# Re-laying the first chunks of an mLSTM cell that feeds a squared-ReLU FFN

## The chip, the cores and the metric

The kernel runs on one core of a Trainium2 chip, as one program. The metric is the device time of one execution in microseconds (us). The engines that matter are TensorE (PE in the profile, with its weight loads as PEld), VectorE (DVE), ScalarE (ACT), GpSimd (POOL) and SyncE (SP), which issues nearly all DMA transfers. Each works through its own instructions strictly in the order in which the kernel lists them, and waits on the others by semaphores.

## The reference

Four sequences with eight heads of 40 elements run through an mLSTM cell over 768 steps. What comes out, 3072 tokens of 320 elements, goes through an FFN with 2048 hidden units.

```python
for t in range(768):                                   # q, k, v, o: (4, 8, 768, 40); gates: (4, 8, 768)
    m_new = max(f[t] + m, i[t])
    f_stab, i_stab, m = exp(f[t] + m - m_new), exp(i[t] - m_new), m_new
    C = f_stab * C + i_stab * outer(v[t], k[t])
    n = f_stab * n + i_stab * k[t]
    y[t] = sigmoid(o[t]) * (C @ q[t]) / max(abs(n @ q[t]), 1)
x = y.transpose(0, 2, 1, 3).reshape(3072, 320)
h = maximum(x @ w_in, 0)                               # w_in: (320, 2048), double precision words
out = (h * h) @ w_out                                  # w_out: (2048, 320)
```

## The kernel before

**Chunks.** The 768 steps of a sequence are cut into six chunks of 128, so there are 24 chunks s in all. Within a chunk the recurrence is a masked, weighted attention, and from chunk to chunk a state C is carried. For each chunk the kernel turns k and q with TensorE (`transposes`, L417, copied out of PSUM in L420), multiplies them (`scores`, L429), forms the weights W as the exponential of a decay row A plus a bias (`weigh`, L391), multiplies scores and weights (`weighted`, L444), and then, in `attend`, multiplies the old state with q (`hi`, L453), forms the new state's addition (`dC`, L460), and multiplies the weighted scores with v (`hp`, L467). `normalise` (L589 to L599) divides by the denominator and applies the output gate, and `turn_rows` (L629, L630) turns the result for the FFN.

**Gates.** A comes from the forget and input gates of all 32 rows (sequence, head) and 768 steps at once: `do_gates` (L252 to L261) runs two scans and six elementwise instructions on VectorE, and `turn_gates` brings the bias `b_T` and the factor `eA_T` into the other layout. A chunk needs A spread over all 128 partitions. For chunks 0 and 1 `spread_A` does that with TensorE: per half of the heads one 512 wide f32 matmul that writes the causal mask (L354) and four 128 wide matmuls that add the rows (L358). From chunk 2 on A goes to DRAM (`a_rows`, L916), comes back by a broadcasting DMA (`A_bc`, L342), and POOL applies the mask (`mask`, L367).

**Rounding of the weights.** w_in and w_out arrive as 64 bit words. Eighteen pieces are fetched through four buffers (`raw`, L193), each fetch being issued when the piece four before it has been joined. A piece takes two ScalarE instructions (`words`: L202, L204), three on VectorE (`join`: L213, L217, L218), and one 32 bit integer addition on POOL (L222). The first FFN group needs pieces 0 to 2, the second 3 and 4, the third 5 to 7, the fourth 8 and 9.

**FFN.** `ffn1_main` (L651) multiplies 256 tokens (two chunks) with 512 columns of w_in, and `ffn1_rest` (L662) adds the last 64 rows; four such groups make one 256 token block. `relu_half` (L675) and `square_half` (L681) follow on ScalarE. Later blocks use forms with fewer products (L742, L816, L848).

**Order.** The order on each engine is written out by hand: a list of calls for the front (L896 to L955), then a loop u = 0 to 7 that mixes chunks 2 to 5 with eight FFN groups, then a loop over all remaining parts. `idle(n)` (L883) issues n matmuls of zeros that nobody reads: twelve at the start, and 4, 3, 4 and 4 later.

```python
    do_gates()
    rounding.words()
    nc.scalar.dma_start(A_d[:, :], A_sb[:])
    spread_A(0)
    ...
    spread_A(1)
    scores(1, (True, True))
```

Of the kernel before, what the change touches and what calls it, by code (L numbers as in the profile page):

```python
# [17 lines left out]
P = 128  # L18
# [11 lines left out]
def kernel(  # L30
# [60 lines left out]
    conv = brought.enter_context(tc.tile_pool(name="conv", bufs=2, side="right"))  # L91

# [18 lines left out]
    later = gates.tile([P, P], F32)  # L111

# [4 lines left out]
    def make_consts():  # L117
        for t in kq_b:
            nc.vector.memset(t[:, :, :, D:], 0.0)
        for t in va_b:  # L120
            nc.vector.memset(t[:, :, D:], 1.0)
        for t in va_w:
            nc.gpsimd.memset(t[:, H * D1 :], 0.0)
        nc.vector.memset(keep[:], 1.0)
        nc.vector.memset(keep[:, :, 0:1], 0.0)
        make_identity(nc, ident[:])

        nc.gpsimd.memset(sel[:], 0.0)
        nc.gpsimd.affine_select(
            sel[:], sel[:], compare_op=ALU.not_equal, fill=1.0, base=0, pattern=[[-1, H], [0, P]], channel_multiplier=1,  # L130
        )

        nc.gpsimd.memset(later[:], 0.0)
        nc.gpsimd.affine_select(
            later[:], later[:], compare_op=ALU.is_ge, fill=-1e30, base=0, pattern=[[1, P]], channel_multiplier=-1,
        )

        nc.gpsimd.memset(bdm[:], 1.0)
        nc.gpsimd.memset(bdm[:DP, :, 1, :], 0.0)
        nc.gpsimd.memset(bdm[DP:, :, 0, :], 0.0)  # L140
# [29 lines left out]
    class Rounding:  # L170
# [36 lines left out]
        def join(self):  # L207
# [14 lines left out]
            nc.gpsimd.tensor_tensor(dst.bitcast(I32), bits, low.bitcast(I32), op=ALU.add)  # L222
# [24 lines left out]
    def load_gates():  # L247
        nc.sync.dma_start(f_sb[:], f_gate.rearrange("b h s -> (b h) s"))
        nc.scalar.dma_start(i_sb[:], i_gate.rearrange("b h s -> (b h) s"))

    def do_gates():
        nc.vector.tensor_tensor_scan(m_sb[:], f_sb[:], i_sb[:], -1e30, op0=ALU.add, op1=ALU.max)  # L252
        nc.vector.memset(f_sb[:, 0:1], 0.0)
        nc.vector.tensor_tensor(f_sb[:, 1:], f_sb[:, 1:], m_sb[:, : S - 1], op=ALU.add)
        nc.vector.tensor_tensor(f_sb[:, 1:], f_sb[:, 1:], m_sb[:, 1:], op=ALU.subtract)
        nc.vector.tensor_scalar_max(f_sb[:], f_sb[:], LOG_ZERO)
        nc.vector.tensor_tensor_scan(
            A_sb[:], keep[:].rearrange("p c t -> p (c t)"), f_sb[:], 0.0, op0=ALU.mult, op1=ALU.add,
        )
        nc.vector.tensor_tensor(i_sb[:], i_sb[:], m_sb[:], op=ALU.subtract)  # L260
        nc.vector.tensor_tensor(i_sb[:], i_sb[:], A_sb[:], op=ALU.subtract)  # L261

    def turn_gates():
        for src, dst in ((i_sb, b_T), (A_sb, eA_T)):
            tp = ps_o.tile([P, W], F32, name="tp", tag="o_ps")[:, : S // P * BH].rearrange("p (c r) -> p c r", r=BH)
            for c in range(NB):
                nc.tensor.transpose(tp[:, c, :], src[:, c * P : (c + 1) * P], ident[:BH, :BH])
            nc.scalar.activation(
                dst[:].rearrange("p b c h -> p c b h"), tp.rearrange("p c (b h) -> p c b h", b=B),
                AF.Copy if dst is b_T else AF.Exp,  # L270
            )
# [74 lines left out]
    def spread_A(s):  # L346

        b, c = divmod(s, NB)
        H2 = H // 2
        d = st.setdefault(s, {})  # L350
        d["A"] = []
        for i in range(2):
            A = ps_h.tile([P, H2, P], F32, name="A_ps", tag="h_ps")
            nc.tensor.matmul(  # L354
                A[:], lhsT=ident[:], rhs=later[:].unsqueeze(1).to_broadcast([P, H2, P]), start=True, stop=False,
            )
            for h in range(H2):
                nc.tensor.matmul(  # L358
                    A[:, h, :], lhsT=sel[:, i * H2 + h, :], rhs=A_sb[:, c * P : (c + 1) * P],
                    start=False, stop=(h == H2 - 1),  # L360
                )
            d["A"].append(A)
# [16 lines left out]
    def weigh(s, masked=False):  # L379
        b, c = divmod(s, NB)  # L380
        d = st[s]
        A, n = d["A"], H // len(d["A"])
        d["W"] = flat_c[:, H * P * (s % 2) : H * P * (s % 2 + 1)].rearrange("p (h t) -> p h t", t=P) if s < W_IN else A[0]
        if s < X_SQ:
            d["dec"] = prep.tile([P, H], F32, name="dec")
        if len(A) == 1 and not masked:
            mask(s)
        for i in range(len(A)):
            hh = slice(i * n, (i + 1) * n)
            for h in range(n):  # L390
                nc.scalar.activation(  # L391
                    d["W"][:, i * n + h, :], A[i][:, h, :], AF.Exp, bias=b_T[:, b, c, i * n + h : i * n + h + 1],
                )
            if s < X_SQ:
                nc.scalar.activation(d["dec"][:, hh], A[i][:, :, P - 1], AF.Exp)
        values(s)
# [14 lines left out]
    def transposes(s, o=(False, False)):  # L411
        d = st[s]
        kqT(s)
        for i, n in enumerate(("kT", "qT")):
# [5 lines left out]
            (nc.scalar.copy if i == 0 or s in (0, *range(2, 7)) else nc.vector.tensor_copy)(d[n], tp)  # L420
# [25 lines left out]
    def attend(s):  # L446
        b, c = divmod(s, NB)
        d = st[s]
        C = st.get("C")
        if c > 0:  # L450
            hi = ps_at.tile([P, H, D1], F32, name="hi", tag="at")
            for j in range(PR):
                nc.tensor.matmul(  # L453
                    hi[:, 2 * j : 2 * j + 2, :].rearrange("p h d -> p (h d)"), lhsT=d["qT"][:, j, :],
                    rhs=C[:, j].rearrange("p h d -> p (h d)"), start=True, stop=True,
                )
        if c + 1 < NB:
            dC = ps_at.tile([P, PR, 2, D1], F32, name="dC", tag="at")
# [6 lines left out]
        hp = d["hp"] = ps_at.tile([P, H, D1], F32, name="hp", tag="at")  # L465
        for h in range(H):
            nc.tensor.matmul(  # L467
                hp[:, h, :], lhsT=d["P"][h % 2][:, h // 2, :], rhs=d["va"][:, h, :], start=True, stop=True,
            )
        d["num"] = hp  # L470
        if c > 0:
            num = d["num"] = old.tile([P, H, D1], F32, name="num", bufs=1)
            nc.vector.tensor_tensor(
                num[:], hi[:], eA_T[:, b, c, :].unsqueeze(2).to_broadcast([P, H, D1]), op=ALU.mult,
            )
        if c + 1 < NB:
            Cn = old.tile([P, PR, 2, D1], F32, name="C_sb")
            nc.vector.tensor_tensor(Cn[:], dC[:], bdm[:], op=ALU.mult)
            if c > 0:
                Cd = old.tile([P, H, D1], F32, name="Cd", bufs=1)  # L480
                nc.gpsimd.tensor_tensor(
                    Cd[:], C[:].rearrange("p j i d -> p (j i) d"),
# [4 lines left out]
            st["C"] = Cn  # L487

# [96 lines left out]
    def normalise(s):  # L585
# [4 lines left out]
        dm = work.tile([P, H], F32, name="dm")  # L590
# [3 lines left out]

        x = d["x"] = work.tile([P, 3 * P], F32, name="x_sb")
        x3 = x[:, :DM].rearrange("p (h d) -> p h d", d=D)
        nc.vector.tensor_tensor(x3, num[:, :, :D], d["og"], op=ALU.mult)
        nc.vector.tensor_tensor(x3, x3, dm[:].unsqueeze(2).to_broadcast([P, H, D]), op=ALU.mult)
        nc.vector.tensor_copy(x[:, DM:], x[:, DM - KR : DM])  # L599

# [39 lines left out]
    def ffn1_main(g, pp):  # L640

        if pp == 0:
            new_g2(g)
        xT = st["xT", g]

        hs = [ps_h.tile([P, 2, WG], F32, name="h_ps") for _ in range(2)]
        for i in range(2):
            for n in range(2):
                fb = 4 * pp + 2 * n + i
                for a in range(2):  # L650
                    nc.tensor.matmul(  # L651
                        hs[i][:, n, :], lhsT=w_in[:, a, fb * P : (fb + 1) * P], rhs=xT[:, :, a, :],
                        start=(n == 0 and a == 0), stop=False,
# [225 lines left out]

    def idle(n):  # L880
        t = ps_h.tile([P, W], F32, name="idle", tag="h_ps")
# [14 lines left out]
    load_gates()  # L896
    load_part(0, 0)
    load_part(0, 1)
    fetch(2)
    make_consts()  # L900
    load_part(1, 0)
    load_part(1, 1)
    load_part(0, 2)
    fetch(1)
    load_o(0)
    load_o(1)
    load_part(1, 2)
# [3 lines left out]
    idle(4)  # L911
    scores(0)
    idle(3)
    do_gates()
    rounding.words()
    nc.scalar.dma_start(A_d[:, :], A_sb[:])  # L916
    spread_A(0)
    rounding.words()
    turn_gates()
    rounding.join()  # L920
    weigh(0)
    transposes(1, (False, True))
    spread_A(1)
    scores(1, (True, True))
    weigh(1)
    first.close()
    ffn = ctx.enter_context(tc.tile_pool(name="ffn", bufs=2))
    before = ExitStack()
    old = before.enter_context(tc.tile_pool(name="old", bufs=2))
    weighted(0)  # L930
    weighted(1)
    load(2)
# [5 lines left out]
    attend(0)  # L938
    rounding.step()
    normalise(0)  # L940
    mask(2)
    attend(1)
    normalise(1)
    load(3)
    load_A(3)
    rounding.step()
    turn_rows(0)
    idle(4)
    transposes(2)
    idle(4)  # L950
    sigmoid(2)
    sigmoid(3)
    turn_rows(1)
    weigh(2, masked=True)
    rounding.step()  # L955
# [3 lines left out]
    for u in range(8):  # L959
        s = 2 + u // 2  # L960
        relu_half()
        if u % 2 == 0:
            if u == 0:
                ffn1(0, 0)
                scores(s)
                rounding.step()
            else:
                turn_rows(s - 1)
                scores(s)
                ffn1(u // 4, u % 4)  # L970
            if u == 2:
                rounding.words()
# [7 lines left out]
            else:  # L980
                weigh(s + 1)
                square_half()
        else:
            load_A(s + 2)
            for r in {1: (4,), 3: (5, 6), 5: (7,), 7: ()}[u]:
                load(r)
# [4 lines left out]
            if u == 3:  # L991
                square_half()
# [12 lines left out]
            square_half()  # L1005
# [5 lines left out]
    square_half()  # L1011
# [134 lines left out]
```

## Time and profile before

| | |
|---|---|
| median of 12 runs | 514.0 us (512.96 to 515.07) |
| the profiled execution's own time | 515.07 us |
| its span, first to last instruction | 513.3 us |
| PE busy / PEld busy | 504.3 us / 462.4 us |
| DVE, ACT, POOL busy | 346.9, 248.4, 113.6 us |
| mean granted TensorE clock | 0.992 |

The profiled execution is the slowest of the twelve. Outside its span lie 515.07 - 513.3 = 1.77 us. A row of the timeline gives the start, the length, the engine, the line, what is written and read, the number of like instructions merged, and in brackets how long the engine had been idle and what ended that. In a table of stretches each row is a piece of the span with the busy time of each engine in it, the share of the TensorE clock that was granted (PEclk), and the use of the DMA engines. PE's busy time counts a matmul until its result is out, so a busy PE isn't PE at its peak. All times in the text are counted from the start of the span.

### The profile page before, as it was taken

To read this page: it belongs to the slowest core of one execution; us is meant where nothing else is said; L and a number is where in the kernel's file an instruction comes from. 1 tells how busy PE (TensorE), PEld (TensorE's weight loads), DVE (VectorE), ACT (ScalarE), POOL (GpSimd) and SP (SyncE) were. 2 spreads that over 40 slices of the span, in tenths; PEclk is the share of its full clock that TensorE was granted. 3 is DMA by queue.
4 is the path that set the end of the run, shared out by engine and by line. 5 is a ranking of instruction groups with operands and counts; after the bars stand their busy time and mean duration, and the time that the engine had idled before them with its cause. 6 is when DMAs were issued, how large, how long until landed. Compare 5 with 4: busy or idle time off the path is not lost.

```text
span 513.3 us, 11843 instructions
## 1 busy us (share of the span) xinstructions
PE 504.3 (98%) x4649; PEld 462.4 (90%) x4649; DVE 346.9 (68%) x630; ACT 248.4 (48%) x492; POOL 113.6 (22%) x138
## 2 busy tenths in 40 slices
PE   9989999999999999999999999999999999999997
PEld 4868878787798999999999999999999999999997
DVE  8589866663879776668668767667669667644341
ACT  3767888745440641680651780550771641432400
POOL 3345643232013122112112131112112112020000
PEclk9997999999999999999999999999999999999999
DMA  9999899845574785685675785785755353100000
GB/s 194 219 220 204 247 234 185 166 105 107 119 162 91 177 157 113 167 158 116 161 144 110 182 151 112 175 162 92 172 122 113 96 115 86 44 10 28 0 27 27
DMA packets 238231, 67.63 MB, mean 132 GB/s; under 512 B 185600, under 2 KB 232704, under 8 KB 238176
## 3 DMA queue, kind: packets, MB, share of 16 engines
q1 hardware_dynamic: 238080, 66.68, 62.0%
q8 instruction: 37, 0.61, 0.5%
q10 hardware_dynamic: 96, 0.20, 0.1%
q14 instruction: 18, 0.15, 0.1%
HBM read 54.56 MB, written 17.86 MB: 141 GB/s over the span
## 4 chain that ended last, share of the span: by engine, by line
PE 89%; DVE 4%; DMA 2%; issue 2%; ACT 1%; SPq 1%; DVEq 0%
PE h_ps L742 32%; PE h_ps L816 21%; PE h_ps L651 7%; PE h_ps L848 7%; PE tp L429 4%; PE h_ps L688 3%; PE numT L528 3%; PE h_ps L662 2%; PE hp L467 2%; PE numT L519 2%; DMA A_bc<-a_rows 1%; PE tp L417 1%; PE dC L460 1%; PE A_ps L358 1%; PE dC L538 1%
## 5 line engine op out<-in xcount | busy, mean ns | idle before, releaser
L367 POOL TENSOR_SCALAR_AFFINE_SELECT A_bc<-A_bc 128x1024 f32<-128x1024 f32 x22 | 27.7, 1258 | 212.2 <-ACT kq L377 136.2
L742 PE MATMUL h_ps<-T,S 128*128 128x160 f32 x352 | 51.4, 299 | 0.0
L391 ACT ACTIVATE A_bc<-A_bc,b_T 128x128 f32<-128x128 f32 x144 | 44.0, 388 | 10.8 <-POOL A_bc L367 10.4
L742 PE MATMUL h_ps<-w_out,g 128*128 128x160 f32 x336 | 49.2, 303 | 0.0
L742 PEld LDWEIGHTS h_ps<-T,S 128*128 128x128 f32 x352 | 49.0, 190 | 0.0
L377 ACT ACTIVATE kq<-A_bc 64x512 f32<-64x512 f32 x30 | 18.9, 629 | 61.7 <-DMA A_bc<-a_rows 61.5
L651 PE MATMUL h_ps<-xT,w_in 128*128 128x256 f32 x192 | 45.7, 394 | 1.6 <-ACT xT L630 1.6
L742 PEld LDWEIGHTS h_ps<-w_out,g 128*128 128x128 f32 x336 | 46.1, 190 | 1.1
L651 PEld LDWEIGHTS h_ps<-xT,w_in 128*128 128x128 f32 x192 | 36.9, 197 | 7.6 <-ACT xT L630 2.0
L816 PE MATMUL h_ps<-xT,w_in 128*128 128x128 f32 x288 | 40.7, 285 | 0.5 <-ACT r_sb L829 0.5
L829 ACT COPY r_sb<-h_ps 128x512 f32<-128x512 f32 x18 | 10.5, 584 | 61.3 <-PE h_ps L816 61.3
L758 DVE TENSOR_TENSOR y_sb<-y_sb,h_ps 128x160 f32<-128x160 f32 x44 | 14.0, 319 | 36.2 <-PE h_ps L742 36.2
L816 PE MATMUL h_ps<-xs,w_in 128*128 128x128 f32 x288 | 38.1, 275 | 0.0
L816 PEld LDWEIGHTS h_ps<-xT,w_in 128*128 128x128 f32 x288 | 34.9, 191 | 3.5 <-ACT r_sb L829 0.7
L848 PE MATMUL h_ps<-xT,w_in 64*128 64x128 f32 x432 | 36.9, 281 | 0.0
L848 PEld LDWEIGHTS h_ps<-xT,w_in 64*128 64x128 f32 x432 | 33.4, 188 | 2.2
L816 PE MATMUL h_ps<-xs,WS 128*128 128x128 f32 x288 | 35.1, 275 | 0.0
L816 PEld LDWEIGHTS h_ps<-xs,w_in 128*128 128x128 f32 x288 | 35.0, 192 | 0.0
L816 PEld LDWEIGHTS h_ps<-xs,WS 128*128 128x128 f32 x288 | 33.6, 192 | 0.0
L853 DVE TENSOR_TENSOR r_sb<-r_sb,h_ps 128x512 f32<-128x512 f32 x18 | 12.4, 687 | 26.7 <-PE h_ps L848 26.7
L545 DVE STREAM_TRANSPOSE tn<-numT 128x256 f32<-128x256 f32 x36 | 15.8, 449 | 21.1 <-PE numT L528 21.1
L444 DVE TENSOR_TENSOR A_bc<-tp,A_bc 128x512 f32<-128x512 f32 x36 | 23.1, 684 | 9.5 <-PE tp L429 9.5
(168 smaller groups left out, 1069.5 us busy)
## 6 DMA issues: line engine op xcount, KB each, us to landing
A_bc<-a_rows SPq DMA_DIRECT2D x22, 512.0 KB, 4.7
raw<-in_moe_w_out_dram SPq DMA_DIRECT2D x8, 640.0 KB, 4.4
num_rows<-tn SPq DMA_DIRECT2D x18, 256.0 KB, 3.5
kq<-num_rows SPq DMA_DIRECT2D x72, 64.0 KB, 2.5
kqT<-kq_rows SPq DMA_DIRECT2D x34, 128.0 KB, 3.2
raw<-in_moe_w_in_dram SPq DMA_DIRECT2D x8, 512.0 KB, 5.5
kq<-in_k_dram SPq DMA_DIRECT2D x24, 160.0 KB, 5.0
va<-in_v_dram SPq DMA_DIRECT2D x24, 160.0 KB, 5.1
```

The lines of the kernel that those rows point to most:

```text
L367: nc.gpsimd.affine_select(A[:], A[:], compare_op=ALU.is_ge, fill=-1e30, base=0, pattern=[[0, H], [1, P]], channel_multiplier=-1,)
L377: nc.scalar.activation(e[rows], st[s]["A"][0][rows, PR * i : PR * (i + 1), :], AF.Exp)
L391: nc.scalar.activation(d["W"][:, i * n + h, :], A[i][:, h, :], AF.Exp, bias=b_T[:, b, c, i * n + h : i * n + h + 1],)
L429: nc.tensor.matmul(sc[i][:, j, :], lhsT=d["kT"][rows, j, :], rhs=d["qT"][rows, j, :], start=True, stop=True,)
L444: nc.vector.tensor_tensor(t, d["sc"][i], d["W"][:, heads, :], op=ALU.mult)
L528: nc.tensor.matmul(numT[i][halves[g], e, :], lhsT=va_w[s % NKQ][:, h * D1 : h * D1 + DP], rhs=d["P"][h % 2][:, h // 2, :] if s < KQ_SQ els ...
L545: nc.vector.transpose(to[:, 2 * i : 2 * i + 2], numT[i][:, :2, :].rearrange("p c t -> p (c t)"))
L651: nc.tensor.matmul(hs[i][:, n, :], lhsT=w_in[:, a, fb * P : (fb + 1) * P], rhs=xT[:, :, a, :], start=(n == 0 and a == 0), stop=False,)
L688: nc.tensor.matmul(o_ps, lhsT=st["g2", g][:, fb, j * P : (j + 1) * P], rhs=w_out[:, fb, :], start=(fb == 0), stop=(fb == NF - 1),)
L742: nc.tensor.matmul(to, lhsT=lhsT[:, p], rhs=rhs[:, p, :], start=(start and p == 0), stop=(p == NPAIR - 1), skip_group_check=True,)
L816: nc.tensor.matmul(to[:, n, :], lhsT=lhsT[:, 4 * q + n, :], rhs=rhs, start=(start and n == 0), stop=True, skip_group_check=True,)
L848: nc.tensor.matmul(to[:, n, :], lhsT=w_in2[rows, 4 * q + n, :], rhs=rhs, start=False, stop=True, skip_group_check=True,)
```

## The change

The work per chunk and per weight piece stays the same; what changes is the order of the first four chunks and how some steps are done.

- The gates are computed and loaded in two parts (`SPANS`): first the 256 steps of chunks 0 and 1, then the other 512, with one elementwise instruction less. Each part is stored to `a_rows` by itself, now from SP's queue, not ACT's.
- Chunk 0's A is still spread by TensorE, but the mask matmul is in bf16. Chunk 1's A comes by `load_A(1)` and `mask(1)`, as for later chunks; its ten matmuls go. Both copies of `transposes` are always on ScalarE.
- `attend` and `normalise` are cut into pieces, which the front calls one by one; `weigh` can be done in two halves.
- The first FFN group is multiplied in two halves of 128 tokens, chunk 0's before chunk 1's.
- The fillers stand elsewhere: twelve at the start, then 3, 2, 1, 2, 2 and 2, all into one PSUM bank.
- The rounding's last step goes from POOL to VectorE. There it becomes one instruction over 16 bit halves: 128x1024 elements for a piece of 512 words, 128x1280 for one of 640.
- Weight pieces are fetched later in SP's queue (piece 0 behind the first store of A, piece 1 behind `load_A(1)`), and the loop begins at u = 2.

```diff
@@ constants
+    later_h = gates.tile([P, P], BF16)
+    ident_h = gates.tile([P, P], BF16)
+        nc.vector.tensor_copy(ident_h[:], ident[:])
+        nc.vector.tensor_copy(later_h[:], later[:])
@@ join
-            nc.gpsimd.tensor_tensor(dst.bitcast(I32), bits, low.bitcast(I32), op=ALU.add)
+            nc.vector.tensor_tensor(dst.bitcast(I32), bits, low.bitcast(I32), op=ALU.add)
@@ gates
+    FIRST = 2
+    SPANS = (slice(0, FIRST * P), slice(FIRST * P, S))
+    def load_gates(part):
+        cols = SPANS[part]
+        nc.sync.dma_start(f_sb[:, cols], f_gate.rearrange("b h s -> (b h) s")[:, cols])
+        nc.scalar.dma_start(i_sb[:, cols], i_gate.rearrange("b h s -> (b h) s")[:, cols])
+    def gates_floor(part):     # scan, subtract, add, clamp
...
+    def gates_sum(part):       # scan, one max-and-add
...
+    def turn_gates(part):
...
@@ spread
+    def spread_mask(s):
+        d = st.setdefault(s, {})
+        d["A"] = [ps_h.tile([P, PR, P], F32, name="A_ps", tag="h_ps") for _ in range(2)]
+        for A in d["A"]:
+            nc.tensor.matmul(
+                A[:], lhsT=ident_h[:], rhs=later_h[:].unsqueeze(1).to_broadcast([P, PR, P]), start=True, stop=False,
+            )
+    def spread_A(s, i):
...
@@ transposes
-            (nc.scalar.copy if i == 0 or s in (0, *range(2, 7)) else nc.vector.tensor_copy)(d[n], tp)
+            nc.scalar.copy(d[n], tp)
@@ attend
+    def attend(s):
+        from_C(s)
+        to_C(s)
+        from_chunk(s)
+        decayed(s)
+        next_C(s)
@@ normalise
+    def normalise(s):
+        denominators(s)
+        gated(s)
@@ ffn1_main
-    def ffn1_main(g, pp):
+    def ffn1_main(g, pp, half=None):
...
+                        hs[i][:, n, cols], lhsT=w_in[:, a, fb * P : (fb + 1) * P], rhs=xT[:, js, a, :],
...
@@ the front, whole up to chunk 2
+    load_gates(0); load_part(0, 0); load_part(0, 1); load_gates(1); make_consts()
+    gates_floor(0); gates_sum(0); load_part(0, 2); load_part(1, 0); load_part(1, 1)
+    store_A(0); fetch(1); load_o(0); load_A(1); load_part(1, 2); fetch(1); load_o(1); fetch(1)
+    idle(12); transposes(0); spread_mask(0); idle(3); spread_A(0, 0); turn_gates(0); idle(2)
+    spread_A(0, 1); idle(1); scores(0); weigh(0); gates_floor(1); mask(1); weighted(0); gates_sum(1)
+    load_part(2, 0); load_part(2, 1); store_A(1); fetch(1); transposes(1, (True, True))
+    rounding.words(); from_chunk(0); idle(2); to_C(0); turn_gates(1)
...
+    rounding.join(); denominators(0); next_C(0); idle(2); scores(1, (True, True))
+    rounding.words(); weigh(1, masked=True); rounding.join()
+    load_part(2, 2); load_A(2); load_o(2); load_o(3); sigmoid(0); sigmoid(1)
+    rounding.words(); weighted(1); to_C(1); from_C(1); from_chunk(1); idle(2)
+    gated(0); decayed(1); turn_rows(0); mask(2); transposes(2); normalise(1); next_C(1)
+    ffn1_main(0, 0, 0); rounding.words(); turn_rows(1)
...
+    scores(2); ffn1_main(0, 0, 1); ffn1_rest(0, 0, st["half"][0])
...
-    for u in range(8):
+    for u in range(2, 8):
```

(In the front above several calls share a line; in the file each has its own.)

## Prediction

> **What bounds the kernel now.** I first read the page's busy shares and its 40 slices, then a table of stretches, then the timeline of the first 70 us.
>
> ```profile
> PE 504.3 (98%) x4649; PEld 462.4 (90%) x4649; DVE 346.9 (68%) x630; ACT 248.4 (48%) x492; POOL 113.6 (22%) x138
> ```
>
> PE is busy nearly throughout. So the question is at which time PE gets into the dense part, and what it does before that. The stretches:
>
> ```profile
> 15.00:21.00 6.00, 6.00 (x44) 4.12 (x43) 2.49 (x4) 5.05 (x21) 1.19 (x2) 1.00 1.08 249
> 21.00:30.00 9.00, 8.74 (x71) 7.54 (x70) 8.32 (x20) 5.97 (x12) 4.25 (x5) 1.00 1.14 213
> 30.00:41.00 11.00, 8.82 (x65) 7.59 (x66) 8.98 (x15) 6.84 (x16) 5.72 (x5) 1.00 0.92 197
> 41.00:48.00 7.00, 7.00 (x28) 6.37 (x28) 6.25 (x12) 6.80 (x17) 4.12 (x5) 0.52 1.29 228
> 48.00:62.00 14.00, 14.00 (x102) 11.68 (x102) 12.21 (x19) 10.93 (x24) 8.52 (x8) 1.00 0.77 232
> ```
>
> The third number is PE, the fifth DVE, and the third from the end the granted clock. From 41 us on PE is always busy, with a few us idle in the remaining 450 (70 to 95 us: 25.00 of 25.00). From the third FFN group on both kernels issue the same matmuls, so what the front gains or loses by then is the change in the time. Second, from 21 us to 62 us DVE is the other full engine: 8.32 + 8.98 + 6.25 + 12.21 = 35.8 of 41 us. Third, between 41 and 48 us PE ran at half its clock. The timeline shows what went before that, and what DVE does there:
>
> ```profile
> 39.46 1.09 PE L460 MATMUL dC<-vw,kq 128*128 128x82 f32 x8 [1.07 <-DVE g_c L444]
> 40.39 2.76 PE L467 MATMUL hp<-va,g_c 128*128 128x41 f32 x16
> 42.95 1.95 PE L417 MATMUL tp<-ident,kq 128*128 128x128 f32 x8
> ...
> 49.48 1.32 POOL L222 TENSOR_TENSOR w_in<-mag,low 128x512 int32<-128x512 int32 x1 [1.72 <-ACT mag L202]
> 49.70 1.38 DVE L217 TENSOR_SCALAR mag<-mag 128x512 int32<-128x512 int32 x1
> ```
>
> PE stood idle for 1.07 us, with small matmuls on both sides, and about 2 us later L417 took 1.95 us where it took 1.09 us at 14.13. And L217, which takes 0.43 us alone (12.33), takes 1.38 us when it starts under a POOL addition. The forms of DVE's groups give the sum (the first 70 us):
>
> ```profile
> L217 DVE TENSOR_SCALAR mag<-mag 128x512 int32<-128x512 int32 x10 | 8.1, 808 | 0.3
> L218 DVE SCALAR_TENSOR_TENSOR mag<-raw,mag 128x512 int32<-128x512 int32 x10 | 6.9, 692 | 0.3
> ```
>
> Ten L217 cost 8.1 us where 10 x 0.43 = 4.3 would do, so POOL's additions cost DVE 3.8 us here, and 0.95 us more at L599 (46.65, 1.15 us against 0.20): 4.75 us.
>
> **The change, part by part.** *TensorE's share.* Chunk 1's spread goes (1.02 + 1.16 + 1.13 + 1.15 = 4.5 us), and chunk 0's two f32 mask matmuls (1.02 and 1.13) become two bf16 ones, at 0.22 each by the fillers of the same shape (four in 1.03 with the drain): 1.7 us less. The halves of the first FFN group cost nothing: 8 half-wide products take about 1.9 us (L816, 16 records in 1.95) against 3.72 for 8 full ones. Three fillers fewer: 0.7 us. About 6.9 us of PE work go, but I credit none of it in the main sum, since by my ledger DVE sets when PE may go on; if DVE didn't, it would count in full (first rival).
>
> *Chunk 1's weights.* This is a new path, and the longest. The gates' loads are there by about 3.9 us (L252 started at 4.06 with all columns; DVE is free at 3.5 and has two small copies more). Part 0 takes a third of 1.75 + 0.94 + 0.95 + 0.55 + 1.75 us, with some fixed time: 2.3 us; A is ready at 6.2. Then the store and the load, each from issue to landing; the first 30 us have rows for both:
>
> ```profile
> A_bc<-a_rows SPq DMA_DIRECT2D x2, 512.0 KB, 5.3
> a_rows<-A_sb ACTq DMA_DIRECT2D x1, 96.0 KB, 4.1
> ```
>
> 6.2 + 4.1 + 5.3 = 15.6 us. POOL's mask takes 1.1 (L367), so 16.7. But ACT has piece 1's `words` ahead of `weigh(1)`, and piece 1 is now fetched behind `load_A(1)` and chunk 1's v, issued at about 11.7; with 5.6 us to landing (raw, same stretch) it is there at 17.3, two instructions of 0.6 make 18.5, eight exponentials 2.45 (L391 at 32.92), POOL's vw 0.74: 21.7 us. Now PE: `scores(1)` needs the bank that the copies of `turn_gates(1)` free. Part 1 of the gates ends on DVE at about 14.6 (6.2 + 0.35, five instructions worth 5 us, weighted(0) 1.29, two waits), its turns 0.5, the copies 0.5, then eight products of 1.16: PE is through at about 17.6. Next in its order is dC of chunk 1, which needs vw at 21.7. So PE idles for some 4.1 us (bounds: 2 us if the DMAs take the minimum of 3.9 and the store 2.5; 6 us with the A_bc maximum of 6.3), and no filler stands there: the two before `scores(1)` are done by then. Before, A_ps matmuls filled this place (15.05 to 19.3).
>
> *The clock.* In before a window with 1.07 us of idle PE lost the clock for 6.7 us. I take it that 4.1 us lose it too, and that it stays away while dC, hi and hp run. These three took 1.09 + 1.12 + 1.92 = 4.13 us at full clock; L417's 1.95 against 1.09 gives 1.79, so 3.3 us more. Bounds: 0 (the clock stays) and twice that (6.6, a second loss further on). The Trainium skill ("TensorE: Matmul & The Clock Gate", Why this matters for your kernels) asks only that PE not idle for over about 3 us between bursts. By it the 1.07 us before should have cost nothing, but the clock fell; the row is stricter than the page, and at 4.1 us both lose the clock, so the sum is the same by either. At 2 us they would part: the page's sum would be 3.3 us lower.
>
> *VectorE's ledger.* I follow DVE to the first instruction of piece 2's join, L213 at 30.62 in before. After: dC starts at 21.7, plus 4.13 is 25.8; `normalise(1)` without stalls is 0.50 + 0.17 + 0.17 + 0.20 + 0.47 + 0.49 + 0.20 = 2.2, then C_sb 0.49: 28.5. That is 2.1 us ahead of before. The joins of pieces 0 and 1, with their additions, lie in the wait for chunk 1 (DVE is idle half of 15 to 21 us even now). If that cover were gone they would cost 1.4. The lost clock turns -2.1 into +1.2.
>
> From there on each of pieces 2 to 9 has an addition on DVE. No row shows it. L218, two operands over the same 512 words, took 0.69; L737, two operands and 1024 elements, 1.22. I take 0.69, since the bytes are L218's: 8 x 0.69 = 5.5 us. The Trainium skill ("VectorE: DVE Perf Modes", Mode 2×_1P) says that adjacent 16 bit elements go two a cycle, which is the lower of my ends; by one a cycle the sum would be 4.2 us higher. Gone are POOL's 4.75 us of stalls. Net +0.75. POOL keeps mask, vw and the two state steps (1.1, 0.74, 0.73, 0.88 a chunk), and the additions are more DVE work that can start under one: nothing to three chunks of 0.9, so 0 to 2.7; I take 0.8, a third.
>
> *At nothing.* The qT copy moved to ACT (0.69 off DVE early, in idle time). Two table loads more on ACT (1.28 each): ACT waits for POOL's masks there (41.20: 3.47 idle); 2.6 us if not. The second store, and SP's order: while SP waits for A it holds the k, o and weight loads behind it; the weights come later, but piece 2 lands by about 20.5, long before 28. The later squares have all of blocks 0 and 1 as cover.
>
> *The sum.* +1.2 + 0.75 + 0.8 = +2.75 us at the state of chunk 3 (L473, 58.42 before), which gates the fourth FFN group's transposes; from there PE carries it to the end. On the profiled execution 515.07 + 2.75 = 517.8; that run is 1.07 above the median, so 514.0 + 2.75 = **516.8 us**.
>
> **The rivals.** *Faster: chunk 1's weights come early.* If store and load take their minima and the clock stays, dC starts 2 to 3 us sooner and nothing halves: -5.1 + 0.75 + 0.8 = -3.6. If DVE also isn't the pacing engine, PE's own ledger holds: -6.9, less the 3.3 us of lost clock that before pays, plus the wait of 4.1 that remains: about -6. So 508 to 512, centre 510.4. For it: PE was busy in before wherever DVE was. Against it: every DMA of the first 30 us took 5 us or more, in a stretch where the DMA share is over 1. It decides at an idle stretch ahead of dC of about 1.1 us, the length that cost the clock before. Chance 0.25.
>
> *Level: the idle stretch is as I say but costs no clock* (the window falls well, or the work around it suffices): -2.1 + 0.75 + 0.8 = -0.55, so 513.5. Against it is the 1.07 us that were enough. Chance 0.13.
>
> *Much slower: the addition goes one half at a time,* 1.22: +2.75 + 4.2 = 521. Against it: instruction form and bytes of L218. Chance 0.07.
>
> **How the numbers follow.** The forecast has 0.55: its own range is 515.2 (no new stalls, wait a little shorter) to 519 (three chunks of stalls, or a second short loss of clock). To leave out no more than 2 in 10 the range goes down to 510.4, which drops half of the faster case (0.12), and up to 519.4, which drops the slow addition (0.07). A measurement of this kernel can tell 0.2%, 1.03 us, from no change. Slower by more: 0.55 + 0.07, less 0.03 of the forecast's low end: 0.59. Within: 0.13. Faster: 0.25 + 0.03: 0.28.
>
> **What would show it.** In the profile after: a row for dC of chunk 1 with some 4 us idle before it, released by POOL's vw, and half clock in the stretch behind it; DVE's 128x1024 instruction at about 0.69; no L217-like row at 1.38 that starts under an addition; A_bc(1) landing near 15.6. I'm wrong if PE shows no gap over 1.1 us between 17 and 22 us, if the granted clock stays at 1.00 up to 40 us, or if the second and third FFN groups start several us earlier and the fourth does too.

## The result

The changed kernel takes 517.37 us (median of 11 runs, 515.71 to 522.71), the kernel before beside it 513.85 (47 runs). By the medians it is 3.5 us slower. The ratio, here and below, is one of means (executions over 1.5% above the quickest of their kernel left out): 1.0088, 95% interval 1.007 to 1.0106, slower by 3.6 to 5.4 us, since the longest executions raise the mean. The eleven times lie in two groups: seven from 515.7 to 517.6 at a mean granted clock of 0.980 to 0.987, four from 520.3 to 522.7 at 0.967 to 0.970. The profiled execution (517.22 us, span 515.3) is of the first group. On its page PE is busy 2.1 us less, DVE 4.6 more, POOL 23.5 less. PE's 2.1 isn't the work that went: at half clock what is left takes longer, and half clock lasts longer than before:

```profile
PE 502.2 (97%) x4640; PEld 463.0 (90%) x4640; DVE 351.5 (68%) x654; ACT 251.0 (49%) x496; POOL 90.1 (17%) x121
```

The stretches (third number PE, fifth DVE, third from the end the granted clock), to be held against those of before:

```profile
15.00:21.00 6.00, 3.61 (x37) 2.76 (x34) 5.62 (x12) 3.18 (x11) 1.38 (x1) 1.00 1.10 215
21.00:30.00 9.00, 7.28 (x34) 7.00 (x35) 3.77 (x8) 4.17 (x9) 0.74 (x1) 0.58 1.09 264
30.00:41.00 11.00, 10.63 (x82) 9.12 (x80) 10.21 (x21) 8.71 (x18) 2.92 (x3) 0.88 1.05 212
...
48.00:62.00 14.00, 11.36 (x86) 9.77 (x85) 13.21 (x25) 12.04 (x30) 4.94 (x5) 1.00 1.02 250
62.00:70.00 8.00, 7.81 (x37) 6.09 (x37) 5.64 (x13) 3.26 (x6) 3.11 (x4) 0.79 1.20 232
```

PE now idles where it was full (15 to 21 us, and 48 to 62 us), and behind each of the two the clock falls. The timeline has the first:

```profile
15.34 1.38 POOL L396 TENSOR_SCALAR_AFFINE_SELECT A_bc<-A_bc 128x1024 f32<-128x1024 f32 x1 [2.49 <-DMA A_bc<-a_rows]
...
18.29 0.67 ACT L208 ACTIVATE mag<-raw 128x512 f32<-128x512 f32 x1 [0.89 <-DMA raw<-in_moe_w_in_dram]
...
19.41 2.43 ACT L420 ACTIVATE g_c<-A_bc,b_T 128x128 f32<-128x128 f32 x8
...
22.72 2.00 PE L491 MATMUL dC<-vw,kq 128*128 128x82 f32 x8 [4.11 <-POOL vw L433]
...
24.51 1.92 PE L481 MATMUL hi<-C_sb,kqT 128*128 128x82 f32 x8
...
26.22 3.55 PE L502 MATMUL hp<-va,g_c 128*128 128x41 f32 x16
```

These are the steps of the new path: mask behind the DMA, the words of piece 1 ahead of the exponentials, then vw, and dC after 4.11 us of idle PE. dC and hp take twice what they took before. The second place:

```profile
61.65 0.48 DVE L511 TENSOR_TENSOR num<-hi,eA_T 128x328 f32<-128x328 f32 x1
...
62.19 1.09 PE L447 MATMUL tp<-ident,kq 128*128 128x128 f32 x8 [2.20 <-DVE num L511]
...
63.12 5.30 PE L708 MATMUL h_ps<-xT,w_in 128*128 128x256 f32 x16
```

The transposes of chunk 4 wait 2.20 us for chunk 3's num on DVE; the FFN matmuls behind them take 5.30 us, against 3.62 at full clock in before. The clock's record gives half rate from 22.50 us on for 10.24 us and from 63.46 on for 3.41; in before it is 6.83 us from 41.25 on.

**The front carries all of it.** From the fifth FFN group's first matmul to the end of the execution, these profiled executions need the same within 0.7 us:

| kernel | fifth group starts | profiled execution | rest |
|---|---|---|---|
| before | 68.50 | 515.07 | 446.6 |
| after | 71.03 | 517.22 | 446.2 |
| before_fill | 67.18 | 513.03 | 445.9 |
| before_add | 69.53 | 515.38 | 445.9 |
| fill20 | 66.16 | 512.50 | 446.3 |
| add_pool | 72.42 | 518.62 | 446.2 |
| weigh_first | 71.67 | 517.64 | 446.0 |
| fill_join_early | 74.43 | 520.60 | 446.2 |

Of the other six, five need 446.1 to 446.4; fill_weigh_first needs 447.6, with the clock at half from 66.81 to 70.22 us, across that point. So what follows is about the first 70 us alone.

### The profile page after: what moved, and what is told of

The parts are those of the page before. It is cut to its first block, busy times and chain, and to the rows that moved or that the text cites. A ratio compares the mean times of both kernels' runs of the same rounds, so it can differ in the third digit from the quotient of the medians.

```text
span 515.3 us, 11859 instructions
## 1 busy us (share of the span) xinstructions
PE 502.2 (97%) x4640; PEld 463.0 (90%) x4640; DVE 351.5 (68%) x654; ACT 251.0 (49%) x496; POOL 90.1 (17%) x121
## 4 chain that ended last, share of the span: by engine, by line
PE 87%; DVE 5%; issue 3%; ACT 2%; DMA 2%; POOL 1%; DVEq 0%; POOLq 0%
PE h_ps L799 32%; PE h_ps L873 22%; PE h_ps L905 7%; PE h_ps L708 7%; PE numT L577 4%; PE tp L459 4%; PE h_ps L745 3%; PE h_ps L719 2%; PE numT L568 2%; PE hp L502 1%; DMA A_bc<-a_rows 1%; PE dC L587 1%; PE tp L447 1%; PE hi L481 1%; DVE mag L224 1%
## 5 line engine op out<-in xcount | busy, mean ns | idle before, releaser
L396 POOL TENSOR_SCALAR_AFFINE_SELECT A_bc<-A_bc 128x1024 f32<-128x1024 f32 x23 | 29.0, 1260 | 241.7 <-ACT kq L406 189.2
L708 PE MATMUL h_ps<-xT,w_in 128*128 128x256 f32 (+1 forms) x208 | 46.2, 377 | 1.6 <-ACT xT L685 1.1
```

The costliest lines, as they stand in the source:

```text
L396: nc.gpsimd.affine_select(A[:], A[:], compare_op=ALU.is_ge, fill=-1e30, base=0, pattern=[[0, H], [1, P]], channel_multiplier=-1,)
L708: nc.tensor.matmul(hs[i][:, n, cols], lhsT=w_in[:, a, fb * P : (fb + 1) * P], rhs=xT[:, js, a, :], start=(n == 0 and a == 0 and not half), ...
```

## Experiments

In each line the median is of 6 (add_pool, early_fills) or 12 runs, the ratio is against the kernel before on the same chip. "Fillers" are `idle(n)`, n matmuls of zeros. Theory: PE's idle stretches lose the clock, and that is most of the 3.5 us. Main rival: the additions on VectorE are.

### Fill the idle stretch: fill20

```diff
     weighted(1)
+    idle(20)
     to_C(1)
```

> Twenty fillers on zeros (0.21 us each at full clock, 4.2 us) stand on TensorE ahead of dC of chunk 1, where it idled 4.11 us. Theory (the idle stretch loses the clock, and the slow dC, hi and hp hold up VectorE): the granted clock stays at 1.00 from 22 to 32 us, dC to the end of hp takes about 4.1 us again instead of 7.05, normalise(1) starts some 2.9 us sooner (about 27), and the time falls by 2 to 3 us, to 514.3 to 515.4; not the whole 2.9, since VectorE has later work of its own. Rival A (the additions on VectorE and its stalls under POOL are the whole cost): the clock comes back but the time stays at 517. Rival B (it is the idle time as such, the late weights): no change either, and the next FFN groups start when they did.

Measured: 514.81 (512.5 to 520.49), ratio 1.0011 (0.9992 to 1.003): 2.6 us less than after. Its profiled execution, the quickest of the twelve, never loses the clock:

```profile
21.00:30.00 9.00, 8.86 (x68) 7.33 (x67) 6.82 (x18) 6.00 (x13) 1.21 (x1) 1.00 0.94 243
...
48.00:62.00 14.00, 11.52 (x77) 9.92 (x76) 13.08 (x25) 13.37 (x32) 5.05 (x5) 1.00 1.04 245
```

dC starts at 23.07, no sooner than in after, but hp ends near 26.7 instead of 29.8. The weights of chunk 1 come as late as in after, so most of the cost was not the wait itself but the clock lost in it. Ten of the other eleven executions took 513.0 to 515.8 at 0.993 to 1.000.

### The addition back on POOL: add_pool

```diff
-            nc.vector.tensor_tensor(dst.bitcast(I32), bits, low.bitcast(I32), op=ALU.add)
+            nc.gpsimd.tensor_tensor(dst.bitcast(I32), bits, low.bitcast(I32), op=ALU.add)
```

> The changed kernel with the rounding's addition back on POOL, nothing else. Theory: VectorE loses 8 x 0.69 = 5.5 us of additions after piece 1 and gets stalls under POOL's additions back, 4.75 us in the kernel before; the lost clock from 22 to 32 us stays. So the time falls by 0.5 to 2 us, to 515.2 to 516.7. Rival A (the additions are the whole cost): 513.9 or less. If it comes out above 517.2, the addition on VectorE was a gain by itself.

Measured: 522.6 (518.62 to 525.05), ratio 1.015 (1.0107 to 1.0194), 5 us more than after by the medians. These six lie in two groups too, and only two are in the quicker one (518.62 and 518.87) against seven of eleven in after. Group against group, or profile against profile (518.62 against 517.22), it is 1.4 to 2.6 us more. Both sides of the expectation were wrong but for its last sentence. In its profile:

```profile
38.41 1.32 POOL L228 TENSOR_TENSOR w_in<-mag,low 128x512 int32<-128x512 int32 x1 [1.16 <-DVE mag L224]
41.52 0.74 POOL L433 TENSOR_TENSOR vw<-va,g_c 128x328 f32<-128x328 f32 x1 [1.78 <-ACT g_c L420]
42.22 1.27 POOL L228 TENSOR_TENSOR w_in<-mag,low 128x512 int32<-128x512 int32 x1
```

POOL works strictly in order. The addition of piece 4 was ready when its last operand was, near 40.7, but stood behind vw, which waited for ACT; it began at 42.22, and the second FFN group waited for it:

```profile
43.54 4.73 PE L708 MATMUL h_ps<-xT,w_in 128*128 128x256 f32 x14 [2.91 <-POOL w_in L228]
```

The clock fell once more in it (at 43.07 us). In the new order the addition on VectorE is a gain.

### The addition alone: before_add

The kernel before with the same line on `nc.vector`.

> The kernel before with the rounding's addition on VectorE, nothing else. Theory: the addition's net price is 0.75 us, with new stalls under POOL's remaining work 0 to 2.7, so 514.6 to 516.6 against 513.9; the clock is lost once, near 41 us, as before, or somewhere near it. Rival A (the additions are the whole cost of the change): 517 or more. If the ten stalls under POOL's additions were dearer than the additions themselves: below 513.9.

Measured: 515.45 (514.62 to 516.46), ratio 1.003 (1.0013 to 1.0048), 1.5 us more than 513.97. In the old order, then, the addition costs what the prediction's two terms (0.75 + 0.8) gave it. It is not the whole cost: the rival asked for 3.5.

### A shorter idle stretch: weigh_first

```diff
-    rounding.words()
     weigh(1, masked=True)
+    rounding.words()
+    weighted(1)
     rounding.join()
...
     rounding.words()
-    weighted(1)
     to_C(1)
```

> ACT does weigh(1) ahead of words of piece 1, and VectorE weighted(1) ahead of piece 1's join. The exponentials start at about 17.4 (copies of turn_gates(1) done) instead of 19.41, vw ends at 20.8 instead of 22.66, and TensorE idles about 2.2 us ahead of dC of chunk 1 instead of 4.1. Theory (an idle of over about 1.1 us is enough to lose the clock): the clock still falls, dC to hp still takes about 7 us, but all of it 1.9 us sooner; the time falls by 1 to 2 us, to 515.2 to 516.2. Rival C (idle under 3 us costs no clock): the clock stays at 1.00 to beyond 28 us and the time falls by 3.5 to 5 us, to 512.3 to 513.8. Rival A (additions): 517.

Measured: 515.83 (514.68 to 522.93), ratio 1.0039 (1.002 to 1.0059), 1.5 us less than after.

```profile
20.30 0.74 POOL L433 TENSOR_TENSOR vw<-va,g_c 128x328 f32<-128x328 f32 x1 [4.22 <-ACT g_c L420]
...
21.09 2.00 PE L491 MATMUL dC<-vw,kq 128*128 128x82 f32 x8 [1.99 <-POOL vw L433]
...
24.59 3.55 PE L502 MATMUL hp<-va,g_c 128*128 128x41 f32 x16
```

The clock was lost all the same, for 13.65 us, and everything came 1.6 us sooner, which is what the time shows. But the idle stretch of 1.99 us wasn't the cause by itself. It begins at 19.10, when `scores(1)` is through, and the clock fell at 19.77, after 0.67 us of it:

```profile
16.36:19.77 3.41, 2.63 (x29) 1.85 (x28) 3.13 (x9) 2.32 (x9) 0.00 (x0) 1.00 1.08 210
19.77:23.19 3.42, 2.10 (x10) 2.10 (x11) 3.22 (x7) 3.39 (x8) 0.74 (x1) 0.50 1.06 112
```

In the 3.41 us before the fall PE ran 2.63 us: the 32-row turns of the gates, two fillers and the 40-row scores. Rival C, that the clock stays while no idle stretch is over 3 us, is refuted. So the rule in the Trainium skill ("TensorE: Matmul & The Clock Gate", Why this matters for your kernels), no gap of over about 3 us between bursts of matmuls, is too lenient here.

### Chunk 1's gates by TensorE again: spread_1

```diff
-    load_A(1)
...
     scores(0)
+    spread_mask(1)
+    spread_A(1, 0)
+    spread_A(1, 1)
     weigh(0)
+    weigh(1)
     gates_floor(1)
-    mask(1)
...
     rounding.words()
-    weigh(1, masked=True)
     rounding.join()
```

> Undoes one part of the change: chunk 1's gates are spread by TensorE again (two bf16 mask matmuls and eight f32 matmuls, 2.7 us behind scores(0)), without load_A(1), POOL's mask(1) and the wait for the DMA; weigh(1) follows weigh(0) on ACT. Theory: vw is ready at about 18 to 19 us and TensorE has no idle stretch of over about 1 us ahead of dC of chunk 1, so the clock stays there without a filler and the time is that of the fillers, 514 to 515.5; if the new order leaves a wait of 2 us for weighted(1), half of that more. Rival (the DMA route is a gain by itself, 2.7 us less on TensorE, and the loss is the additions'): 517 to 520.

Measured: 515.26 (514.58 to 515.86), ratio 1.0017 (1.0005 to 1.0028), 2.1 us less than after. dC of chunk 1 follows without idle at 20.96, but the next wait takes its place. hp is released by `gated(0)` (L648, 24.51 to 24.99, which reads chunk 0's hp from PSUM), and on VectorE that stands behind piece 1's join (from 20.96) and `weighted(1)` (23.31):

```profile
25.04 2.98 PE L502 MATMUL hp<-va,g_c 128*128 128x41 f32 x16 [2.07 <-DVE x_sb L648]
```

2.07 us idle, and 6.83 us at half clock behind them. The clock fell once more, at 49.69 us, and there PE had hardly idled: 3.21 of the 3.42 us before are busy, the longest gap is 0.20, and the matmuls are small ones (hi, dC, hp, scores):

```profile
46.27:49.69 3.42, 3.21 (x32) 2.93 (x32) 3.21 (x7) 3.39 (x7) 0.92 (x1) 1.00 0.98 255
49.69:53.10 3.41, 3.41 (x10) 2.69 (x9) 3.14 (x8) 3.34 (x11) 1.21 (x2) 0.50 0.97 141
```

So without the DMA route the kernel is 2.1 us quicker although TensorE has 2.7 us more to do. What the route cost was mostly the uncovered wait: with fillers over it the DMA route takes 514.81 (fill20), and 513.17 with a second place filled (next). This run with its own wait filled wasn't measured, so which route is better with the clock kept stays open.

### Fillers in the second place too: fill_two_places

```diff
     weighted(1)
+    idle(20)
     to_C(1)
...
+            if u == 3:
+                idle(10)
             transposes(s + 1)
```

> Twenty fillers ahead of dC of chunk 1 and ten (2.1 us) ahead of the transposes of chunk 4, where TensorE idled 2.20 us in the profile with the first twenty. Theory (each idle of more than about 1.1 us may lose the clock, and most executions lose it at this second place): the times draw together at 512.5 to 513.5, with a mean granted clock of 0.997 or more in each. Rival (the clock is lost elsewhere, or the second stretch of idle costs nothing): median 514.8 with clocks of 0.993 as before.

Measured: 513.17 (512.28 to 519.5), ratio 0.9995 (0.9969 to 1.0021). Ten of twelve lie between 512.3 and 514.1 at a clock of 0.999 or 1.000; two (517.2, 519.5) ran at 0.993 and 0.984; where they lost the clock wasn't profiled. By the medians that is 1.6 us less than with the first fillers alone (the two intervals overlap), and the clocks of 0.993 to 0.997 that most executions of fill20 had are gone: the second idle stretch is the other cause. From after to here 4.2 us went with fillers alone.

### Sooner weights and fillers: fill_weigh_first, two_fills_weigh_first, three_fills_weigh_first

`weigh_first` with ten fillers ahead of dC; then with ten ahead of chunk 4's transposes as well; then also three, three and none in the places among the gates' matmuls where after has two, one and two.

> Two edits together: weigh(1) on ACT and weighted(1) on VectorE go ahead of piece 1's words and join, as in the run before (515.83), and ten fillers (2.1 us) stand ahead of dC of chunk 1. Theory: the clock stays at 1.00 to 32 us as with twenty fillers (514.81), and dC starts about 1.9 us sooner than there (near 21.1 instead of 23.07), so 1 to 2 us less than 514.81: 512.8 to 513.8. Rival (with the clock kept VectorE's joins alone set the end, and chunk 1 may come when it will): 514.8.

> Fillers in two places (ten ahead of dC of chunk 1, ten ahead of the transposes of chunk 4), and weigh(1) and weighted(1) ahead of piece 1's words and join. Theory: with the clock kept the earlier weights of chunk 1 (1.9 us) carry through to chunk 3's num, so 1 to 1.9 us less than with the fillers in two places alone (513.17): 511.3 to 512.2, apart from 2 or 3 executions of 12 near 518 to 520 that lose the clock near 11 us. Rival (VectorE's joins alone set the end): 513.2.

> As the run before in this list, with the early fillers too (three and three among the gates' matmuls, none ahead of to_C(0)). Theory: the same median, 511.3 to 512.4 (scores(0) comes 0.6 us later, of which little reaches the end), and no execution above 515; so this beats the kernel before (514). Rival (VectorE's joins alone): 513.2. Rival (the long times come from elsewhere): 2 to 3 of 12 still at 518 or more.

Measured: 514.97 (513.27 to 520.77), 513.86 (512.15 to 515.67), 513.9 (512.66 to 516.24); ratios 1.003 (0.9999 to 1.0062), 0.9999 (0.9981 to 1.0017), 1.0008 (0.9991 to 1.0025). The expected further 1 to 2 us did not come, and none of the three beats the kernel before. The medians don't tell what sooner weights are worth with the clock kept, since it wasn't: in two_fills_weigh_first seven of twelve executions ran at 0.993 or less, in fill_two_places one at 0.993 and one at 0.984; the profile of fill_weigh_first has three losses of 3.41 us, that of three_fills_weigh_first one of 6.83 us from 18.06 on. Three profiled executions kept it throughout. In them dC of chunk 1 starts at 23.07 (fill20), 23.02 (fill_two_places) and 21.28 (two_fills_weigh_first), and chunk 3's num at 58.32, 59.34 and 58.62. The first two run the same code up to there, so sooner weights show no gain beyond that scatter of 1 us. That fits the rival here, that later work sets the end, but doesn't show it.

### VectorE's join moved into a wait: fill_join_early

```diff
+    idle(20)
     to_C(1)
...
     gated(0)
+    rounding.join()
     decayed(1)
...
     load_A(3)
-    rounding.join()
     rounding.words()
```

> Twenty fillers ahead of dC of chunk 1, and piece 2's join (0.41 + 0.43 + 0.69 + 0.69 = 2.2 us of VectorE) moved from behind normalise(1) to the place between gated(0) and decayed(1), where VectorE idled 0.49 + 1.25 us with the fillers alone. Theory (from normalise(1) on VectorE paces the front, the additions on it): 1 to 1.7 us less than with the fillers alone (514.81), so 513.1 to 513.8, and chunk 3's num starts 1 to 1.7 us before 58.32. Rival (TensorE's work and the clock pace it): 514.8.

Measured: 517.29 (515.07 to 522.28), ratio 1.0074 (1.0044 to 1.0104): 2.5 us slower than fill20 instead of 1 to 1.7 faster. The profile is of a 520.60 us execution that lost the clock already at 11 us, for 17.07 us, so its time can't be laid beside fill20's. Up to there the two kernels are the same, so that loss isn't the edit's doing, and the medians say little of the edit. But even the executions at a clock of 0.997 (515.07 to 516.03) are no quicker than fill20's at 0.997 (514.29 to 515.05). The theory that VectorE's sum of work from `normalise(1)` on is what paces the front is at best borne out in part. In the profiles that stretch, from L638 of chunk 1 to L511 of chunk 3, is 31.9 us in after (29.80 to 61.65), 31.6 in fill20 (26.77 to 58.32), and 30.7 here (34.40 to 65.06): 2.2 us taken out of it shortened it by 0.9. What takes up the rest stays open.

### The early loss: early_fills

```diff
     turn_gates(0)
-    idle(2)
+    idle(3)
     spread_A(0, 1)
-    idle(1)
+    idle(3)
     scores(0)
...
     from_chunk(0)
-    idle(2)
     to_C(0)
```

> The changed kernel with fillers moved and added among the matmuls of the gates: three instead of two ahead of spread_A(0, 1), three instead of one ahead of scores(0), none instead of two ahead of to_C(0). Nothing stands ahead of dC of chunk 1. Theory (in some executions the clock is lost already near 11 us, where TensorE runs eight 32-row matmuls and four small transposes with few fillers; the profile of the run with the early join shows this): the times of 520 to 523 (4 of 11 executions of the changed kernel) disappear, and the others stay: all at 515.5 to 518, median 517, since the idle of 4.1 us is still there. Rival (the long times come from a further loss behind 60 us, or from something else): 3 to 5 of 12 still at 520 or more.

Measured: 518.07 (516.91 to 523.01), ratio 1.01 (1.0065 to 1.0135). Of six times one is 519.65 and one 523.01, so the longer group is still there and this theory is not supported. That some executions lose the clock near 11 us is seen in one profile (fill_join_early); that after's times of 520 to 523 come from it stays open, since none of those was profiled.

### The kernel before, its own idle filled: before_fill

```diff
# attend, between hi and dC
+        if s == 2:
+            idle(5)
         if c + 1 < NB:
             dC = ...
```

> The kernel before with five fillers (1.07 us) ahead of dC of chunk 2, in the place where TensorE stood idle for 1.07 us at 39.46 and lost the clock at 41.3. Theory (the idle of 1.07 us was the cause): the clock stays at 1.00 through 41 to 48 us, the mean granted clock is 0.997 or more in nearly all executions, and the time falls by 0.5 to 1.2 us, to 512.8 to 513.5. Rival (the many small matmuls are the cause, the idle is not): the clock still falls near 41 us, 514.

Measured: 513.01 (512.28 to 514.03), ratio 0.9983 (0.997 to 0.9996). All twelve executions ran at a clock of 0.999 or 1.000; those of before that count beside them had 0.989 to 0.999.

```profile
38.65 1.25 PE L885 MATMUL idle<-zeros 128*128 128x512 bf16 x5
39.89 1.09 PE L462 MATMUL dC<-vw,kq 128*128 128x82 f32 x8
40.82 1.92 PE L469 MATMUL hp<-va,g_c 128*128 128x41 f32 x16
42.56 1.07 PE L417 MATMUL tp<-ident,kq 128*128 128x128 f32 x8
```

hp takes 1.92 us instead of 2.76, the transposes 1.07 instead of 1.95. The small matmuls are still there and don't lose the clock by themselves in this place; with 1.07 us of idle among them they had, and that cost the kernel before about 0.9 us (0.2 to 1.5). Five fillers make it quicker than both kernels: 4.4 us less than after, 0.9 less than before.

## Why the prediction was right, point by point

517.37 lies in the range (510.4 to 519.4), 0.6 us from the forecast of 516.8. The mechanism is shown. That the forecast came so near is partly luck: several terms were off, some by 2 to 3 us, and they nearly cancelled.

**PE's 6.9 us credited at nothing: right.** Filled in two places, the changed kernel takes 513.17, and before with its one place filled 513.01: with the clock kept, the two fronts are level. The work removed came back as 4.11 + 2.20 = 6.3 us of idle.

**The path of chunk 1's weights: right in its main number.** The idle stretch was 4.11 us (4.1). dC started at 22.72, not 21.7. The store took 2.8 and the load 5.7 us, less than 4.1 + 5.3:

```profile
a_rows<-A_sb SPq DMA_DIRECT2D x1, 32.0 KB, 2.8
```

```profile
9.62 5.66 DMA A_bc<-a_rows
```

(The first is from the DMA issues of the first 30 us, the second from the chain of waits: start, length.) But A was ready at 6.8 instead of 6.2, the mask took 1.38, and piece 1 landed at 18.29, not 17.3. TensorE was a microsecond later as well, so the stretch came out as worked, by two errors that cancelled.

**The lost clock: right in kind, too small in size.** dC to the end of hp took 7.05 us instead of 4.13, +2.9 for the 3.3 of the sum. What the sum left out: half rate lasted 10.24 us, beyond hp, and the clock was lost again behind a second stretch of idle, at 60 us. The prediction had that only as the upper end of its own range. By the medians, filling the first stretch gave 2.6 us, the second 1.6. That idle costs the clock was taken from one stretch of 1.07 us; weigh_first and spread_1 show that its length isn't the rule.

**VectorE up to piece 2's join:** +1.76 (32.38 against 30.62) for +1.2. dC started a microsecond later than worked, which is more than the 0.56 that is missing.

**Additions and stalls: the sum right, each term wrong.** Two joins of after, one stalled, one free:

```profile
33.38 0.84 DVE L223 TENSOR_SCALAR mag<-mag 128x512 int32<-128x512 int32 x1
34.26 1.27 DVE L224 SCALAR_TENSOR_TENSOR mag<-raw,mag 128x512 int32<-128x512 int32 x1
35.67 0.69 DVE L228 CUSTOM_DVE_ANT_0 w_in<-mag,low 128x1024 uint16<-128x1024 uint16 x1
...
37.20 0.69 DVE L224 SCALAR_TENSOR_TENSOR mag<-raw,mag 128x512 int32<-128x512 int32 x1
38.02 0.69 DVE L228 CUSTOM_DVE_ANT_0 w_in<-mag,low 128x1024 uint16<-128x1024 uint16 x1
38.63 0.42 DVE L219 TENSOR_SCALAR mag<-mag 128x512 f32<-128x512 f32 x1
```

The addition takes the 0.69 us foreseen, but waits for the result of L224: from L224's start to the next join it is 1.43 us (37.20 to 38.63), 0.82 more than the 0.61 of before (31.54 to 32.15). Eight make 6.6, not 5.5. Added up over the timeline from piece 2's join to chunk 3's num, the excess over each form's free duration was 6.4 us in before, not 4.75, and is still 4.1 in after, not 0.8: the additions start under POOL's mask and state steps, and L648 and L649 do (0.92 and 1.26 against 0.44 and 0.49). The bound of 2.7 was too low. Against that, DVE's waits for other engines fell from 3.3 us to 0.9, which the sum did not count. 6.6 - 6.4 + 4.1 - 2.4 = +1.9; measured +1.5 (29.27 us against 27.80), forecast 0.75 + 0.8 = 1.55.

**Chunk 3's num:** 61.65 against 58.42, +3.2 for +2.75. But in before nothing waited for it, and in after PE stood 2.20 us for it. The prediction named it as the gate without showing such a wait; there was none until the change brought it.

**At nothing:** the run that puts weigh(1) ahead of piece 1's words gained 1.5 us, so piece 1's later fetch was on the path, as the step on chunk 1's weights had it, though the list of things at nothing took the later weights as free. The table loads and the copies on ACT were not tried alone.

**The rivals.** Faster needed a kept clock and early weights. The one profiled execution that had both (two_fills_weigh_first, clock 1.000) took 512.57, the quickest of its twelve 512.15, the median 513.86: not 510.4, the centre of 508 to 512, so its gain was put too high. Level, the idle stretch without the clock's loss, is what fill20 and fill_two_places show: 513.2 to 514.8 for 513.5. One half at a time is refuted by the 0.69.

## What to carry to other kernels

Taking matmuls out of a front in which TensorE waits for a chain turns them into idle, and idle of 1 to 2 us among small matmuls can cost the clock, here for 3.41 or 6.83 us (10.24 behind 4.11 us of idle). So find each such wait in the timeline first and put a few fillers there: five were worth more than the whole rewrite. And price an instruction that moves to another queue in the order it will stand in: the same addition cost 1.5 us on VectorE in the old order, and saved 1.4 or more in the new one.

## What the runs showed of the hardware

- The clock goes in whole windows: the stretches at half rate were 3.41, 6.83, 10.24, 13.65 and 17.07 us, one to five times 3.41. The Trainium skill ("TensorE: Matmul & The Clock Gate", Part 1) has a free-running window of 4096 cycles, 3413 ns; the records agree.
- The falls of one execution lie whole windows apart (after: 22.50 and 63.46 us, 40.96 = 12 x 3.413), and the grid lies differently in each execution: up to its fall at 11.07 us fill_join_early runs the code of fill20, which kept the clock there.
- The length of an idle stretch doesn't decide. The clock fell in or behind stretches of 1.07, 2.07 and 4.11 us, but 0.67 us into weigh_first's 1.99; 2.20 us lost it in after's profile and not in fill20's, at the same place, with 2.14 and 1.94 us of it in one window (fill20's grid reckoned back from the fall at 510.89 us, behind its last instruction). And it fell with hardly any idle: in spread_1 at 49.69 (longest gap 0.20 us), and in fill_join_early at 11.07, behind 3.41 us in which PE was busy throughout, with 32-row matmuls, small transposes and a few fillers. What the falls have in common is that the window before holds small matmuls, idle time, or both; how much is too little, no run measures.
- A 32 bit integer addition as one VectorE instruction over 16 bit halves takes 0.69 us for 512 words and 0.83 for 640, and it starts 0.13 us behind the end of an instruction whose result it needs (37.89 to 38.02).
